# An adaLN transformer block on one core: the order of 2109 operations taken from a priority list, or from a table of the sequence itself

## The chip, the core and the metric

The kernel runs on one core of a Trainium2 chip. A core has a matrix engine (TensorE, PE in the profile, with its weight loads listed apart as PEld), a vector engine (VectorE, DVE), an activation engine (ScalarE, ACT), a general one (GpSimd, POOL), and a queue that mostly issues transfers (SyncE, SP). Each engine works through its own list of instructions strictly in order and waits on semaphores for the others. SBUF is the on-chip memory of 128 partitions, PSUM the accumulator of the matrix engine, in banks of 512 float32 columns.

The metric is the device time of one execution in microseconds (us). The kernel before takes 337.96 us, the median of three runs (336.16 to 338.79).

## The reference

The input x has 2048 tokens of 640 features, in bfloat16. A condition vector c gives six vectors of 640 by one product with a matrix `w_mod`: a shift, a scale and a gate for each of two layer norms.

```python
mod = (silu(c) @ w_mod).reshape(1, 6, 1, -1)
sa, ca, ga, sb, cb, gb = mod[:, 0], ..., mod[:, 5]
h = layernorm(x) * (1 + ca) + sa
x = x + ga * attention(h, wqkv, wo)
h = layernorm(x) * (1 + cb) + sb
x = x + gb * ((sigmoid(h @ w_gate) * (h @ w_up)) @ w_down)
```

The attention has 32 heads of 20 features, is causal, and a query sees the 256 last positions only. The second half has 1536 hidden features.

## The kernel before, in words

The tokens are cut into eight chunks `a` = 0..7 of 256 tokens (two blocks of 128). A chunk goes through these steps; each is a handful of operations of a program that the kernel first builds as a graph and then puts into an order:

- `x`: a block of x is loaded (by SP or ACT, line 603). Layer-norm statistics on DVE (L791, L793), the inverse root on POOL (L796, L798), the normalised block on DVE or POOL (L811, L808). In the first layer norm these operations carry the names `astats`, `apow`, `axh`, in the second `bstats`, `bpow`, `bxh`.
- `atr`, `btr`: the block is turned by a transposing DMA on SP (L818) and then scaled and shifted (`amodu`, `bmodu`, L826 and L827, on DVE, ACT or POOL), giving hT, and in the second half h2T. In chunks 0 and 1 the first turn is done by PE instead (`aptr`, evicted by `ahTe`, L849 and L850).
- `projq`, `projk`, `projv`: three projections of the turned block, in tiles of 320 columns, each five matmuls cut into pieces of two and three. A tile is evicted by ACT or DVE (`evqk`, `evv`, L884 and L885). q and k are turned by a transposing DMA (`qkt`), in chunks 0 and 1 by PE (`qtr`, evicted by `evqt`).
- `score`: 8 or 16 small matmuls into the tile S, which takes four PSUM banks and exists once. ACT takes the exponential of the whole tile (`exp`, L1005); POOL sets masked corners to zero (`mask`, L1013 and L1015). The next `score` needs S back, so it waits for the exponential before it.
- `pvs`: after six score sets (three in chunk 0) the products with V, into two neighbouring banks of M. In most places `pvs` is one PE operation together with the score that follows it. DVE turns, divides and turns back (`tr1`, `recip`, `divide`, `tr2`: L1052, L1057, L1059, L1061); four DMAs write the result to DRAM (`n_ow`), one or two read it back in the wanted layout (`oT`).
- `wo`: the output projection, added to x on DVE (`res1`, L1135), then the second layer norm.
- `mlpg`, `mlpu`: gate and up products over h2T, `tanh` on ACT (L1180), `glu` on DVE (L1182) into hh. `down`: the last product, added on DVE (`res2`, L1201), and `out`, the store.

Ahead of this stands the head: `w_mod` is loaded in quarters `wm0` to `wm3`, and c gives the modulation columns (`modA`, `modb`, `modc`, evicted at L753, L776). `warm` and `fill` are matmuls on zeros. `wos` and `wds` scale the loaded weights by the gates (L1228, L1163); `wd` and the others are loaded once. Part `wm0` and part `wm3` of `w_mod` are put where `wd` is loaded later.

PSUM holds S (four banks) and M, four banks that all other products share: a new tile of M waits until the eviction of the one that held the bank.

**What sets the order.** `Prog.op` records each operation with the engines that may do it, an assumed duration, and what it reads and writes. `Prog.schedule` (before) is a list scheduler: it keeps a simulated clock for each engine, takes the operations that could start soonest, and among those within 0.14 us (PE) or 0.04 us (others) of the earliest it picks the one with the smallest number in the list `PRIO`. It also picks one of the allowed engines and the buffer. The result is one fixed list for each engine; `Prog.emit` writes these lists out with a semaphore wait wherever an operation needs a result of another engine, a landed transfer, or a buffer. So on the chip every engine only follows its list, and an operation whose turn has come blocks all that stand behind it on that engine.

Nearly every PE instruction stands under one line of a helper, L705, and L706 for those with a tile position (scores and `pvs`). L686 and L697 are the `warm` and `fill` matmuls.

## Time and profile before

| what | us |
| --- | --- |
| median of three runs (lowest, highest) | 337.96 (336.16, 338.79) |
| span of the profiled execution | 333.9 |
| median less that span | 4.06 |
| PE busy, matmuls (L705 and L706 and warm-up) | 325.6 |
| ACT busy | 229.3 |
| PEld busy (beside PE) | 232.0 |
| DVE busy | 222.4 |
| POOL busy | 180.5 |
| 90 exponentials, L1005 | 169.1, mean 1.878 each |

The span goes from the first instruction of the program to its last; 4.06 us separate it from the median of the runs, which were not profiled. An engine is busy when it executes an instruction, not when it waits. The chain is followed back from the last instruction, at each step to what released it. A line of the chain or of the timeline gives the start and the duration in us, then engine, line and tiles (out<-in), and behind `<-` who ended the idle time before it.

### The profile page before, as it was taken

The numbers are of one execution on the slowest core, as the hardware profiler recorded it, in microseconds if no ns is written. First come the engines' busy times: TensorE is split into PE (matmuls) and PEld (weight loads), VectorE is DVE, ScalarE is ACT, GpSimd is POOL, SyncE is SP. The second block draws the span as 40 slices with busy tenths as digits, with TensorE's granted clock in tenths as the row PEclk, the third lists the DMA queues.
The fourth block names the chain that finished last, engine by engine and source line by source line (L and its number), as shares of the span: only waits on it lengthen the run. The fifth ranks groups of instructions, "written<-read, shape, count | busy, mean of one in ns | idle before, by whom it ended". The sixth has DMA issues, their size and how long they took to land.

```text
span 333.9 us, 10066 instructions
## 1 busy us (share of the span) xinstructions
PE 325.6 (98%) x4142; PEld 232.0 (69%) x4142; DVE 222.4 (67%) x445; ACT 229.3 (69%) x218; POOL 180.5 (54%) x259
## 2 busy tenths in 40 slices
PE   7899989998999999999999999999999999999996
PEld 2667646665786667766776776776776777887885
DVE  5389987999969845874486638465856295746323
ACT  1597977878768787888689967895695869221220
POOL 5038988996468764656565656665454667001000
PEclk9999999999999999999999999999999999999999
DMA  7999998984653773047125501501320303102101
GB/s 239 380 375 313 239 261 178 289 187 74 120 97 80 120 124 89 23 101 101 66 61 105 100 26 42 117 22 43 71 67 22 104 2 77 42 24 61 41 0 39
DMA packets 72694, 37.73 MB, mean 113 GB/s; under 512 B 46538, under 2 KB 71370, under 8 KB 72650
## 3 DMA queue, kind: packets, MB, share of 16 engines
q1 hardware_dynamic: 71056, 35.31, 43.9%
q10 hardware_dynamic: 1594, 1.80, 1.7%
q8 instruction: 32, 0.52, 0.6%
q14 instruction: 12, 0.10, 0.1%
HBM read 20.97 MB, written 5.24 MB: 79 GB/s over the span
## 4 chain that ended last, share of the span: by engine, by line
PE 86%; DVE 6%; DMA 3%; issue 2%; SPq 1%; ACT 0%; DVEq 0%
PE M L705 70%; PE S L706 8%; PE M L706 6%; DMA wd<-in_w_mod_dram 3%; PE S L686 2%; SPq L603 1%; DVE st L791 1%; DMA x<-in_A_x_dram 1%; DVE Tn L1059 1%; DVE T L1052 1%; DVE On L1061 1%; DVE x L811 1%; PE S L705 1%; DVE stg L885 1%; DVE h2T L827 0%
## 5 line engine op out<-in xcount | busy, mean ns | idle before, releaser
L1005 ACT ACTIVATE E<-S 128x2048 bf16<-128x2048 f32 x90 | 169.1, 1878 | 44.5 <-PE S L706 42.7
L1013 POOL TENSOR_SCALAR_AFFINE_SELECT E<-E 128x512 bf16<-128x512 bf16 (+2 forms) x90 | 78.2, 869 | 40.2 <-ACT E L1005 40.1
L1015 POOL TENSOR_SCALAR_AFFINE_SELECT E<-E 128x512 bf16<-128x512 bf16 (+1 forms) x84 | 68.5, 815 | 47.7 <-ACT E L1005 44.4
L705 PE MATMUL M<-h2T,wg 128*128 128x256 bf16 x480 | 64.8, 273 | 1.0 <-DVE h2T L827 1.0
L705 PE MATMUL M<-h2T,wu 128*128 128x256 bf16 x480 | 65.2, 273 | 0.0
L1182 DVE SCALAR_TENSOR_TENSOR hh<-sig,M 128x512 bf16<-128x512 f32 x48 | 32.6, 681 | 44.4 <-ACT sig L1180 24.4
L705 PE MATMUL M<-wd,hh 128*128 128x320 bf16 (+2 forms) x396 | 58.4, 295 | 0.0
L705 PEld LDWEIGHTS M<-h2T,wg 128*128 128x128 bf16 x480 | 45.0, 98 | 10.6 <-issue 2.3
L705 PEld LDWEIGHTS M<-h2T,wu 128*128 128x128 bf16 x480 | 45.3, 98 | 9.4 <-issue 3.0
L1180 ACT ACTIVATE sig<-M 128x512 f32<-128x512 f32 x48 | 28.3, 596 | 29.0 <-PE M L705 29.0
L705 PEld LDWEIGHTS M<-wd,hh 128*128 128x128 bf16 x396 | 37.1, 98 | 14.5 <-issue 1.5
L706 PE MATMUL S<-QT,KT 20*128 20x256 bf16 (+1 forms) x960 | 35.9, 245 | 0.2
L1201 DVE TENSOR_TENSOR x<-M,x 128x320 bf16<-128x320 f32 (+2 forms) x33 | 15.7, 479 | 23.4 <-PE M L705 22.9
L791 DVE BATCH_NORM_STATS2 st<-x 128x6 f32<-128x320 bf16 x64 | 28.3, 475 | 3.6 <-DMA x<-in_A_x_dram 3.5
L1052 DVE STREAM_TRANSPOSE T<-M 128x512 f32<-128x512 f32 x32 | 21.3, 697 | 12.7 <-PE S L706 12.0
L706 PEld LDWEIGHTS S<-QT,KT 20*128 20x128 bf16 x960 | 14.1, 92 | 20.1 <-ACT E L1005 12.1
L705 PE MATMUL M<-wk,hT 128*128 128x320 bf16 x160 | 26.6, 300 | 0.1
L705 PE MATMUL M<-wq,hT 128*128 128x320 bf16 x160 | 25.7, 299 | 0.2 <-issue 0.2
L705 PE MATMUL M<-wv,hT 128*128 128x320 bf16 x160 | 25.3, 300 | 0.1
L705 PE MATMUL M<-wo,oT 128*128 128x320 bf16 x160 | 24.1, 300 | 0.0
L706 PEld LDWEIGHTS M<-E,V 128*32 128x32 bf16 x960 | 20.0, 97 | 4.2 <-issue 2.6
L706 PE MATMUL M<-E,V 128*32 128x256 bf16 (+1 forms) x960 | 22.8, 246 | 0.2 <-issue 0.2
(78 smaller groups left out, 316.5 us busy)
## 6 DMA issues: line engine op xcount, KB each, us to landing
x<-in_A_x_dram SPq DMA_DIRECT2D x20, 160.0 KB
doc<-On SPq DMA_DIRECT2D x64, 40.0 KB
wd<-in_w_mod_dram SPq DMA_DIRECT2D x6, 320.0 KB
wd<-in_B_w_down_dram SPq DMA_DIRECT2D x4, 480.0 KB
wu<-in_w_mod_dram SPq DMA_DIRECT2D x5, 320.0 KB
out_dram<-x SPq DMA_DIRECT2D x10, 160.0 KB
oT<-doc SPq DMA_DIRECT2D x8, 192.0 KB
wg<-in_B_w_gate_dram SPq DMA_DIRECT2D x2, 576.0 KB
```

Of the source, the lines that this page charges most:

```text
L603: return e.dma_start(dst(), src())
L686: ins = e.matmul(p_S.aps[0][:, 3, :], Eall[:, 0, 0:128], Eall[:, 0, 128:640], start=True, stop=True)
L705: return e.matmul(o, l, r, start=st, stop=sp, skip_group_check=True)
L706: return e.matmul(o, l, r, start=st, stop=sp, tile_position=tp, skip_group_check=True)
L791: A("dve", lambda e, g, bi=bi, j=j: e.bn_stats(v(bi * 12 + j * 6, 6), src[bi].ap[:, j * 320:(j + 1) * 320]), 0.48, reads=[src[bi].r()], wr ...
L1005: A("act", lambda e, eng: e.activation(E.ap[:], Sp.ap[:], ACT.Exp, scale=SM_SCALE), 1.876, reads=[Sp.r()], writes=[E.r()], prio=3, tag=f"e ...
L1013: return e.affine_select(ap, ap, pattern=[[0, ap.shape[1]], [1, 128]], compare_op=ALU.is_ge, fill=0.0, base=0, channel_multiplier=-1)
L1015: return e.affine_select(ap, ap, pattern=[[0, ap.shape[1]], [-1, 128]], compare_op=ALU.is_ge, fill=0.0, base=-1, channel_multiplier=1)
L1052: A("dve", lambda e, g, h=h: e.transpose(T1.ap[:, 512 * h:512 * h + 512], X[h].ap), 0.694, reads=[X[h].r()], writes=[T1.r(h)], prio=3.5, t ...
L1180: A("act", lambda e, g, pg=pg, sg=sg: e.activation(sg.ap[:], pg.ap[:], ACT.Tanh, scale=0.5), c_act(512), reads=[pg.r()], writes=[sg.r()], ...
L1182: A("dve", lambda e, g, pu=pu, sg=sg, f0=f0: e.scalar_tensor_tensor(out=hh.ap[:, f0:f0 + 2, :], in0=sg.ap[:].rearrange("p (a b) -> p a b", ...
L1201: A("dve", lambda e, g, ps=ps, bi=bi, c0=c0, n=n: e.tensor_tensor(x1[bi].ap[:, c0:c0 + n], ps.ap[:, 0:n], x1[bi].ap[:, c0:c0 + n], op=ALU. ...
```

## The change

`PRIO` goes, and with it the choice by priority. In its place stands `PLAN`, a table with one number for each of the 2109 operations, in the order in which the scheduler is to place them: the number is 5 times the operation's number plus the engine's (pe, act, dve, pool, sp = 0 to 4). `schedule` walks through the table, and its simulated clock now only serves to choose the buffer of each tile (`place`). Some assumed figures of transfers change as well (a mixed turn between transposing and other transfers, the latency of the first loads and of transposes, the work of three loads); on the chip they can act only through the choice of buffers, since the order is in the table. The functions that issue instructions are the same.

```diff
-        o.prio = PRIO[self.seq] if self.seq < len(PRIO) else prio
+        o.prio = prio
...
-            return max(x.end + x.lat for x in ten.rel)
-
-        def slots_for(o):
...
+            return max(x.end + x.lat for x in ten.ops)
+
+        def take(t, s):
+            ten = t.pool.tenant[s]
+            t.prev = list(t.pool.init[s]) if ten is None else list(ten.rel)
+            t.slot = s
+            t.at = slot_time(t.pool, s)
+
+        def place(t):
+            n = len(t.pool.tenant)
+            free_at = [slot_time(t.pool, s) for s in range(n)]
+            if t.mate is not None:
+                best = min((max(free_at[s:s + 2]), s) for s in range(0, n, 2) if None not in free_at[s:s + 2])[1]
+                for x, s in ((t, best), (t.mate, best + 1)):
+                    take(x, s)
+                    t.pool.tenant[s] = x
+            else:
+                best = min((free_at[s], s) for s in range(n) if free_at[s] is not None)[1]
+                take(t, best)
+                t.pool.tenant[best] = t
+
+        assert sorted(x // 5 for x in PLAN) == list(range(len(self.ops)))
+        for code in PLAN:
+            o, e = self.ops[code // 5], ENGS[code % 5]
...
-PE_EPS = 0.14
-PRIO = [
-    237, 718, 740, 875, 142, 777, 323, 635, 239, 322, 238, 840, 25, 1100, 489, 421, 2052, 27, 111, 30, 29, 31, 28,
...
+PLAN = [
...
-MIXED = 0.39
+MIXED = 1.3
...
-    keep[0], keep[1] = load_x(p_x1, 0, 0), load_x(p_x1, 1, 0, eng="act")
+    keep[0], keep[1] = load_x(p_x1, 0, 0, dlat=2.95), load_x(p_x1, 1, 0, eng="act", dlat=2.95)
...
-    dma(lambda: wo[:], lambda: A_wo.rearrange("(t p) f -> p t f", p=128), 2.25, writes=[R_wo], prio=0.5, tag="wo")
+    dma(lambda: wo[:], lambda: A_wo.rearrange("(t p) f -> p t f", p=128), 2.15, writes=[R_wo], prio=0.5, tag="wo")
...
-        return A("sp", fn, dur, reads=reads, writes=writes, prio=prio, work=work, tag=tag, lat=0.08 + DSAFE, dlat=3.64 if work > 0.5 else 3.40)
+        return A("sp", fn, dur, reads=reads, writes=writes, prio=prio, work=work, tag=tag, lat=0.08 + DSAFE, dlat=3.35 if work > 0.5 else 3.25)
```

The table can be read by the operations' numbers. In the names used above, the lists of the engines then differ as follows at the places that matter below (the digit is the chunk, "x4" four pieces in a row, "|" only a help for the eye).

```
SP before, from the start:
x0 wm0x5 wq wm1 wkx2 x3 x2 wv wm1x2 x5 wm2 wm1 wq wm1 x4 wg0 x6 x7 wm2 wo wg0 wg1x2 atr2x2
n_ow_0x4 wu1x2 wu0 oT_0 wu0 | wm3x2 | x8 x9 atr3 qkt2 n_ow_0x4 ...
SP after:
wm0 x0 wm0x4 wq x2 wq wkx2 x5 x4 x3 wv wm1x5 wm2 wo x7 wm2 x6 | wm3x2 | wg1 wg0x2 atr2x2 wg1
wu1 wu0x2 n_ow_0 x9 x8 wd ...
ACT before: x1, c, tanh of c ...        ACT after: c, x1, tanh of c ...

PE before, from the start:
warmx4 ctr modA warmx3 aptr0 fill modA fill modA aptr0 modA fill modA fill aptr0x2 modA fill aptr0 projq0 ...
PE after:
ctr warmx7 modAx2 fill modAx2 fill aptr0x4 modAx2 fillx3 aptr0 projq0 ...
DVE before: ... astats0x5 c_col astats0 siluc silubc axh0x2 ...
DVE after:  ... c_col siluc silubc astats0x6 axh0x2 ...

PE before, from wo0 to mlpg0:
wo0x8 score1 projk3x3 projq3x2 projk3 score1 projq3x6 score1 projv3x2 projk3x2 projv3x3 score1 projk3x2
projv3x3 score2 projk4x6 projq4x2 pvs1 projv4x6 score2 projv4x2 projq4x5 score2 projq4 mlpg0
PE after:
wo0x4 projq3 wo0 score1 wo0x3 projq3 projk3 score1 projk3x2 projq3 projk3 projq3 score1 projq3x2 projv3
projk3x2 score1 projv3 projq3 projk3x2 projq3 projv3 score2 projv3x5 pvs1 mlpg0
DVE before, the second layer norm of chunk 0:
res1_0x2 bstats0 res1_0 bstats0x3 evqk3 bstats0x2 divide_1 evqk3x2 astats5x3 tr2_1 evqk3 astats5 evv3x2
astats5 evqk3 evv3 astats5 evv3 astats6x2 evqk4 astats6 evqk4 wds bxh0 wds bxh0
DVE after:
res1_0 recip_1 divide_1 res1_0x3 bstats0x6 tr2_1 evqk3x2 bxh0x2
POOL after, there: mask1 bpow0 mask1 bpow0 mask1        SP after, there: n_ow_1 atr4 btr0x2
```

(`ctr` turns c; `c_col`, `siluc` and `silubc` are the steps on DVE from it to the operand of `modA`, L673 to L677.) Of the 2109 operations 128 are on another engine than before, nearly all of them evictions and modulations that two or three engines may do; DVE has 437 operations instead of 445, POOL 260 instead of 247, ACT 212 instead of 217 without transfers.

## The prediction

> **What bounds the kernel now.** I read the page first: busy times, then the span in 40 slices.

> ```profile
> span 333.9 us, 10066 instructions
> PE 325.6 (98%) x4142; PEld 232.0 (69%) x4142; DVE 222.4 (67%) x445; ACT 229.3 (69%) x218; POOL 180.5 (54%) x259
> ...
> PE   7899989998999999999999999999999999999996
> ```

> PE is busy for 325.6 of 333.9 us, the next engine for 229.3. Whatever the order, the same 4142 matmuls remain, so only PE's 8.3 idle us (and waits too short to show as idle) can be won. Where they lie is told by PE's busy time in stretches (start:end, length, then PE busy and its instructions):

> ```profile
> 0.00:5.00 5.00, 3.28 (x8) 1.03 (x8) 2.41 (x9) 1.28 (x1) 3.29 (x25) 1.00 0.60 193
> 10.00:15.00 5.00, 4.16 (x50) 2.83 (x47) 1.45 (x4) 2.82 (x7) 0.00 (x0) 1.00 1.10 377
> 30.00:35.00 5.00, 4.64 (x63) 3.06 (x62) 5.00 (x10) 5.00 (x7) 4.20 (x5) 1.00 1.03 173
> 45.00:50.00 5.00, 3.71 (x32) 2.04 (x30) 3.48 (x10) 3.08 (x2) 4.66 (x6) 1.00 1.08 185
> 80.00:85.00 5.00, 4.02 (x42) 2.18 (x40) 5.00 (x10) 3.50 (x5) 3.12 (x3) 1.00 0.02 7
> 100.00:150.00 50.00, 50.00 (x676) 34.98 (x674) 37.12 (x77) 41.22 (x38) 33.12 (x45) 1.00 0.44 89
> ```

> From 85 us to the last matmul, PE's share is full. All that an order can win lies ahead of 85 us: 1.72 us before the first matmul, then 4.0 in holes; the last 2.5 us follow the last matmul. The waits of PE name the holes (total us, times, longest):

> ```profile
> PE M L705 <- DMA wd<-in_w_mod_dram: 1.3, 1, 1.3
> PE M L705 <- DVE h2T L827: 1.0, 2, 0.6
> PE M L705 <- DVE hT L850: 0.6, 1, 0.6
> PE M L705 <- DVE stg L885: 0.4, 1, 0.4
> ```

> Some waits hide in "busy", since a matmul's shown duration covers its way through the array. The chain shows the pattern of the attention: a score set, other matmuls, the next set.

> ```profile
> 124.81 0.34 PE S L706 x16
> 125.14 2.07 PE M L705 x18
> 127.22 0.33 PE S L706 x8
> ```

> S exists once and its exponential takes 1.878 us (mean of 90), so two sets lie never closer than 2.07 us of other work; this shortest value comes again and again. An order with less than that between two sets makes PE wait.

> **Part by part.** The sum goes against the span of 333.9 us; 4.06 us on top lead to the median of the runs.

> *Nothing for the bulk.* The table reorders pieces; the number of changes of PE between full, score and `pvs` form, counted in both lists, is 184 and 184. Evictions that move between ACT and DVE (128 operations in all) are covered by PE: DVE and ACT have a third of the span free. In 100 to 150 us, with 41.22 of 50 us of ACT busy, PE still lost nothing. I take 0, bounds -0.3 (PE's smallest holes) and +1.

> *The wait for `wm3`: -1.3.* Before, SP issues this part behind the four `n_ow_0`, and so behind DVE's `tr2_0`, which ends at 33.06 in the chain; its last issue is at 38.62, and the matmul on it starts at 47.06 instead of 45.77.

> ```profile
> 38.62 8.39 DMA wd<-in_w_mod_dram
> 47.06 1.12 PE M L705 x7
> ```

> After, SP has it directly behind x7, wm2 and x6, which wait only for PE's turns of chunk 1 (before, these ended at about 21). Even if it again takes the 8.39 us, it is there at some 33 us; PE comes to it after 26.8 us of matmuls counted from the first `projq0`, that is at 39. The row is that of the same transfer, so I take all of it; the other bound is 0.

> *The second layer norm of chunk 0: -0.8.* PE waits twice for h2T:

> ```profile
> 81.68 0.38 PE L705 MATMUL M<-h2T,wg 128*128 128x256 bf16 x2 [0.37 <-DVE h2T L827]
> ...
> 82.89 1.09 PE L705 MATMUL M<-h2T,wg 128*128 128x256 bf16 x8 [0.61 <-DVE h2T L827]
> ```

> Before, PE's list has 20.9 us of work between the last `wo0` piece and `mlpg0`, and the chain still was late: DVE did the last `res1` at 60.58 but `bxh0` (L811) only at 73.41, with casts, a division of 1.40 and a wait of 0.78 for x between them. After, PE has only 11.9 us there: 58 matmuls of 320 columns at 0.136, five score sets, one `pvs` of 1.43. But DVE's list is nearly straight. From the start of the last `wo0` piece: the piece and its hand-over 0.6, DVE not free for `res1` until 1.0, `res1` 0.45, statistics 2.3 (four of 0.475, two of 0.195): 4.3 us. On POOL 0.26, a mask of 0.87 to 1.1, the power 0.71: 6.3. `bxh0` 0.4: 6.7, the second one on DVE beside it. Two transposes of 1.22 in SP's queue: the second is issued at 7.9; from its issue to the first use (76.98 to 80.42) it took 3.4: 11.3. The modulation of two fifths 0.5, split over ACT and DVE: 11.8; the others by 12.4. So it just fits, with some 0.2 left of the 1.0: -0.8. Bounds: -1.0, and +7 if the chain is as slow as before (rival 1).

> *Score sets too close: +0.9.* Counted by matmul rows (0.136 for 320 columns, 0.109 for 256), the new list has places with less than those 2.07 us. Example: `wo0x3 projq3 projk3` between two `score1` is 12 matmuls, 1.63, with the change of form 1.73: 0.34 short. Summed over the list 1.7 us are short, with one place of 0.41 in chunk 0, two of 0.33 in chunk 1, one of 0.21 in chunk 2. The old list had 0.7 short, which its time holds already. Net +1.0; some of it falls on waits for an eviction anyway, so +0.9, bounds 0 and +1.0.

> *The head: -0.4.* c is now loaded first and c's small chain on DVE stands ahead of the statistics; on PE `ctr` stands ahead of all warm-up matmuls. It needs the identity, which POOL had at 3.62 before and now makes after a memset of 0.95 (of Tn) and one of 0.2 to 0.9 (nearest rows: DVE's 0.21, Tn's 0.95): 3.0 to 3.7. So PE starts 1.3 to 2.0 later than at 1.72. That is no loss by itself, for the first needed `modA` waits for its load anyway. The gain: after, the two last `modA` follow each other with no `fill` between, and all transfers ahead of them are the same, so the modulation that ended at 10.92 can end by 0.4 to 0.5 us earlier; and the first two evictions of hT run on ACT and DVE at once, 0.3 more. Against it:

> ```profile
> 1.72 3.59 PE L686 MATMUL S<-E 128*128 128x512 bf16 x8 [1.72 <-DVE E L681]
> 5.60 2.14 PE L686 MATMUL S<-E 128*128 128x512 bf16 x6
> ```

> Single matmuls of 512 columns step by 0.427 us up to 6.88 and by 0.217 from then on, 5.16 us after the first one. If the slow time is counted from the first matmul, it now lasts to 8.5; the fourteen warm-up matmuls alone then end at 8.9 instead of 8.3, the five `modA`, fills and turns (2.5 us of rows) at 11.5: +0.6. If it ends at 6.88 as before, -0.75. Between the two I take -0.4, nearer to the gain, since the loads set the last `modA`.

> [...]

> **Sum:** -1.3 -0.8 +0.9 -0.4 = -1.6. Span 332.3, time 336.4 us, 0.5% under the median. A change of about 1% is what a measurement here can tell from none: the three runs differ by 0.8%.

> **Rivals.** 1, slower: *h2T of chunk 0 comes late.* PE's list gives 9 us less to the chain than before (11.9 instead of 20.9), and everything behind `mlpg0` waits on PE in order. For it: the chain took 22 us before, transposes issued in that stage took long, and POOL's power stands behind a mask that waits for ACT. Against it: DVE's list has no load and no foreign division in the chain. If DVE and SP lose again the 7 us by which `res1` to `bxh0` (12.8) exceeded my 5.4, the 0.8 is gone and 7 come on top: 333.9 - 0.8 + 7 = 340.1, time 344. It decides from 5 us of lateness on (1.6 won plus 3.4, which is 1%). Chance 0.21.

> 2, faster: *PE's holes close wholly.* -0.75 (head) -1.3 -1.0 -0.4 (the wait for stg) -0.3 (the smallest holes) = -3.75, the short score sets falling on waits that both lists have: 330.2, time 334.2. For it: none of the holes is needed by the work. Against: the 1.7 short. Chance 0.22.

> 3, no change: *the won time is lost to evictions.* In 15 to 75 us ACT and DVE are near 4.5 to 5.0 of 5 us busy; M has four banks, and `pvs` needs two neighbours, free at once. One such wait is worth an exponential, 1.9, as an eviction behind it on ACT holds a bank. With that, 333.9 - 1.6 + 1.9 = 334.2, time 338.3. Chance 0.17.

> Forecast 0.40. Each case spreads by about 1% around its time. From these: faster by over 1% (under 334.6) 0.25, within 1% 0.54, slower (over 341.3) 0.21. The range reaches from a full gain less a little, 333.0, to the middle of rival 1, 342.5.

> **What would show it.** PE's wait for the `w_mod` load gone; first `projq0` at 11.9 instead of 12.26; `mlpg0` at about 71 instead of 81.68, with a wait for h2T under 0.3; waits of score weights for the exponential longer than 0.4 us near 22 and 60 us; PE full from 85 us on. It is wrong if PE waits over 2 us for h2T or for a bank, or if holes appear behind 85 us, where the list before had none and I have only counted, not followed, each engine.

## The result and the profile after

| what | before | after |
| --- | --- | --- |
| median of the runs, first comparison (us) | 337.8 (336.08 to 338.79, 6 runs) | 334.54 (333.99 to 334.97, 6 runs) |
| median, second comparison (the batch of `after_again`) | 336.19 (335.53 to 338.78, 23 runs) | 334.76 (333.31 to 335.99, 12 runs) |
| span of the profiled execution | 333.9 | 332.3 |
| time less span | 1.8 to 2.0 | 1.7 to 1.8 |

The ratio after to before is 0.9922, interval 0.9896 to 0.9949, in the first comparison and 0.9951 (0.9933 to 0.9970) in the second: a gain of 0.5 to 0.8%. The forecast was 336.4; the time is 1.9 us lower. The profiled execution of the changed kernel is the shortest of its six: their spans go from 332.3 to 333.2, with a median of 332.8.

The page of the changed kernel, busy times and the span in 40 slices:

```profile
span 332.3 us, 10064 instructions
...
PE 324.6 (98%) x4142; PEld 232.7 (70%) x4142; DVE 217.1 (65%) x437; ACT 226.3 (68%) x213; POOL 185.8 (56%) x272
...
PE   6998999999999999999999999999999999999997
```

PE's busy time in stretches (start:end, length, then PE busy and its instructions):

```profile
0.00:5.00 5.00, 1.95 (x6) 0.84 (x7) 2.20 (x7) 1.49 (x2) 2.68 (x12) 1.00 0.61 191
10.00:15.00 5.00, 4.88 (x54) 3.09 (x51) 3.77 (x9) 2.05 (x4) 0.00 (x0) 1.00 1.11 373
25.00:30.00 5.00, 4.04 (x99) 2.88 (x98) 4.27 (x10) 3.99 (x4) 4.41 (x4) 1.00 0.90 279
30.00:35.00 5.00, 5.00 (x67) 3.82 (x65) 4.36 (x13) 3.75 (x6) 3.71 (x4) 1.00 1.27 347
45.00:50.00 5.00, 5.00 (x57) 3.13 (x55) 4.97 (x10) 4.73 (x6) 3.95 (x6) 1.00 0.90 261
80.00:85.00 5.00, 5.00 (x57) 3.19 (x54) 2.17 (x6) 4.12 (x4) 3.88 (x7) 1.00 1.03 141
```

The holes at 45 and at 80 us (1.3 and 1.0 us before) are closed. A new one stands at 25 to 30. The waits of PE (total us, times, longest) name it:

```profile
PE M L617 <- POOL mhalf L561: 3.0, 1, 3.0
PE M L651 <- DMA hh<-in_w_mod_dram: 1.0, 1, 1.0
PE M L651 <- DVE hT L773: 0.3, 1, 0.3
PE M L651 <- DVE T L998: 0.2, 1, 0.2
```

The wait for `wm3` (tensor wd) and both waits for h2T are gone. The first line is the start, where PE waits for the identity, which POOL makes just ahead of mhalf. The second is new: `modc` needs the second part of `wm2` (tensor hh), whose load SP now issues behind x7, at 23.64 (21.93 before); it lands at 29.23. By the semaphore events of the trace 15 of its 16 parts had landed at 27.43, ahead of PE's turn at 28.3; PE waits for the last one.

To see short waits too, I set each PE operation's distance to the next against the shortest such distance of its form (below: "over the rows"). From the first `projq0` on, before loses 6.1 us so and after 4.9. (The measure is a rough one: it gives 1.2 less from there on, where the two spans, less the earlier `projq0`, differ by 0.9.) The large items: `wm3` 1.45 and h2T 0.54 + 0.77, only before; `wm2` 1.03, only after. Score sets at the shortest distance of 2.38 us cost 0.55 before and 1.2 after (0.40, 0.32 and 0.33 in the three worst places). The first `projq0` starts at 11.58 instead of 12.26. Behind 85 us no hole is to be seen in either.

### The profile page after: what moved, and what is told of

Same layout as the page of the kernel before. It is cut to its first block, busy times and chain, and to the rows that moved or that the text cites. A ratio compares the mean times of both kernels' runs of the same rounds, so it can differ in the third digit from the quotient of the medians.

```text
span 332.3 us, 10064 instructions
## 1 busy us (share of the span) xinstructions
PE 324.6 (98%) x4142; PEld 232.7 (70%) x4142; DVE 217.1 (65%) x437; ACT 226.3 (68%) x213; POOL 185.8 (56%) x272
## 4 chain that ended last, share of the span: by engine, by line
PE 93%; ACT 2%; DMA 2%; DVE 1%; POOL 1%; issue 1%; SPq 0%; POOLq 0%
PE M L651 76%; PE S L652 9%; PE M L652 6%; ACT E L951 2%; DMA hh<-in_w_mod_dram 2%; PE S L632 1%; DVE hT L773 1%; PE S L651 0%; PE S L643 0%; POOL Tn L572 0%; DVE T L998 0%; DVE QT L831 0%; POOL ident L558 0%; POOL stg L569 0%; SPq L549 0%
## 5 line engine op out<-in xcount | busy, mean ns | idle before, releaser
L961 POOL TENSOR_SCALAR_AFFINE_SELECT E<-E 128x512 bf16<-128x512 bf16 (+1 forms) x84 | 67.7, 813 | 56.6 <-ACT E L951 56.3
L959 POOL TENSOR_SCALAR_AFFINE_SELECT E<-E 128x512 bf16<-128x512 bf16 (+2 forms) x90 | 75.9, 854 | 17.4 <-ACT E L951 17.2
L651 PE MATMUL M<-h2T,wu 128*128 128x256 bf16 x480 | 68.5, 273 | 0.2 <-DVE T L998 0.2
L651 PE MATMUL M<-h2T,wg 128*128 128x256 bf16 x480 | 67.8, 273 | 0.0
L651 PE MATMUL M<-wd,hh 128*128 128x320 bf16 (+2 forms) x396 | 57.7, 295 | 0.0
L998 DVE STREAM_TRANSPOSE T<-M 128x512 f32<-128x512 f32 x32 | 21.0, 691 | 12.4 <-PE S L652 11.2
L651 PE MATMUL M<-wq,hT 128*128 128x320 bf16 x160 | 27.4, 299 | 0.5 <-DVE hT L773 0.3
L651 PE MATMUL M<-wk,hT 128*128 128x320 bf16 x160 | 27.4, 300 | 0.0
L651 PE MATMUL M<-wv,hT 128*128 128x320 bf16 x160 | 26.0, 300 | 0.0
L831 DVE CAST stg<-M 128x320 bf16<-128x320 f32 x38 | 17.7, 483 | 10.9 <-PE M L651 10.9
L742 POOL TENSOR_SCALAR st<-st 128x2 f32<-128x2 f32 x16 | 3.7, 234 | 34.9 <-DVE st L739 34.6
(79 smaller groups left out, 335.3 us busy)
```

Source lines behind the costliest of these rows:

```text
L651: return e.matmul(o, l, r, start=st, stop=sp, skip_group_check=True)
L742: A("pool", lambda e, g: e.tensor_scalar(v(28, n), var(), EPS, None, op0=ALU.add), 0.2, reads=[st.r(("m", bi)) for bi in range(n)], writes ...
L831: return e.tensor_copy(dst(), src())
L959: return e.affine_select(ap, ap, pattern=[[0, ap.shape[1]], [1, 128]], compare_op=ALU.is_ge, fill=0.0, base=0, channel_multiplier=-1)
L961: return e.affine_select(ap, ap, pattern=[[0, ap.shape[1]], [-1, 128]], compare_op=ALU.is_ge, fill=0.0, base=-1, channel_multiplier=1)
L998: A("dve", lambda e, g, h=h: e.transpose(T1.ap[:, 512 * h:512 * h + 512], X[h].ap), 0.694, reads=[X[h].r()], writes=[T1.r(h)], prio=3.5, t ...
```

## The experiments

In all edits below except `b_banks` each buffer is held to the one that the edited kernel uses, so that only the order changes. Names that begin with b_ edit the kernel before, with a_ the changed one. The rows `b_table` to `b_ln2` ran beside the first batch of before, `b_wm3b` to `a_oldhead` beside the second, the rest beside the third, each batch on a chip of its own; a ratio compares within its batch. The "low-clock" column counts executions whose mean granted clock (the share of its full clock at which PE was let run) was 0.990 to 0.995 instead of 0.999 or 1.0; the spans are medians of the others.

| run | median time | ratio to before | span at full clock (lowest, highest) | low-clock |
| --- | --- | --- | --- | --- |
| before, three batches | 336.58, 336.37, 336.19 | | 334.25, 334.2, 334.2 (333.6, 335.5) | 20 of 81 |
| b_table | 336.35 | 0.9994 [0.9967, 1.0021] | 334.5 (333.9, 335.1) | 2 of 12 |
| b_banks | 336.50 | 0.9988 [0.9963, 1.0013] | 334.5 (334.0, 335.1) | 2 of 12 |
| b_wm3 | 336.17 | 0.9977 [0.9951, 1.0003] | 334.3 (333.5, 335.5) | 0 of 12 |
| b_ln2 | 335.07 | 0.9945 [0.9917, 0.9974] | 332.95 (332.3, 333.6) | 2 of 12 |
| b_wm3b | 334.54 | 0.9933 [0.9908, 0.9959] | 332.6 (332.3, 333.1) | 0 of 7 |
| a_wm2 | 335.11 | 0.9944 [0.9923, 0.9966] | 333.4 (332.3, 333.9) | 0 of 11 |
| a_lnlate | 340.77 | 1.0116 [1.0083, 1.0148] | none | 6 of 6 |
| a_oldhead | 335.43 | 0.9963 [0.9943, 0.9982] | 333.7 (333.0, 334.5) | 0 of 12 |
| after_again | 334.76 | 0.9951 [0.9933, 0.9970] | 333.05 (331.6, 334.3) | 0 of 12 |
| a_space2 | 336.34 | 1.0003 [0.9981, 1.0025] | 334.65 (333.7, 336.7) | 0 of 12 |
| b_both | 332.85 | 0.9894 [0.9864, 0.9925] | 330.95 (330.9, 331.4) | 0 of 6 |
| b_bothhead | 333.61 | 0.9919 [0.9890, 0.9949] | 331.55 (331.1, 332.4) | 0 of 6 |

### Is it the order at all, and where do the runs of before differ?

`b_table` is the order and the buffers of before, in the new code (`pin` is a list with the buffer of each tile).

```diff
 PLAN = [
-    3, 57, 81, 114, 78, 91, 62, 89, 222, 99, 68, 104, 8, 13, 263, 109, 28, 195, 225, 202, 206, 212, 230, 217, 119,
+    91, 62, 23, 89, 3, 81, 72, 114, 53, 222, 104, 43, 57, 225, 48, 99, 67, 33, 230, 263, 78, 109, 235, 367, 38, 372,
...
-            best = min((free_at[s], s) for s in range(n) if free_at[s] is not None)[1]
+            best = pin[t]
```

> The order and the buffers of the kernel before, written as a table in the new code: every engine's list is that of before. Both theories expect a ratio of 1.000 (0.997 to 1.003), about 337.8 us. What it is to tell apart is where the runs of this order differ (336.1 to 338.8 in six runs). Theory A, they differ inside the span, in waits of the first 85 us: time less span is the same in each run (about 1.7 us, as in all runs of the new order) and the spans go from 334.4 to 337.1. Theory B, they differ outside of the span: the spans all lie within 0.5 us of 333.9 and time less span goes from 2.2 to 4.9.

Measured: ratio 0.9994, so table and code carry nothing. Time less span is 1.8 to 2.0 in every execution, and the spans go from 333.9 to 336.5: theory A. They also fall in two heaps. With a granted clock of 1.0 they end at 335.1, with 0.995 they begin at 336.0. In the 81 executions of before, 20 have the lower clock (spans from 335.7 on, the others up to 335.5).

`b_banks` is the same order with the buffers that the new figures choose.

```diff
-            best = pin[t]
+            best = min((free_at[s], s) for s in range(n) if free_at[s] is not None)[1]
```

> The order of the kernel before, but with the buffers that the new figures choose for it (96 tiles of M lie in another PSUM bank). Theory A, banks carry nothing: 337.8, ratio 0.998 to 1.002. Rival, the new choice of banks is a part of the gain (fewer waits for an eviction): 0.5 to 1.5 us less, 336.3 to 337.3, and PE's stalls by missing banks (33.1 and 75.8 us in the old profile, 0.7 together) gone.

Measured: 336.50, ratio 0.9988. The stalls at 33.1 and 75.8 us stay (0.42 and 0.37 over the rows). The choice of banks is no part of the gain.

### The wait for wm3

First the two loads ahead of the parts of `w_gate`:

```diff
 SP: ... x6 x7 wm2 wo
+wm3 wm3
 wg0 wg1 wg1 atr2 atr2 n_ow_0x4 wu1x2 wu0 oT_0 wu0
-wm3 wm3
 x8 x9 ...
```

> The kernel before with one edit: the two loads of wm3 stand behind wo in SP's queue, ahead of the four parts of w_gate, and no more behind the writes of n_ow_0. Theory A, the wait is a loss of its own: PE's 1.3 us for w_mod at 45.8 is gone and the span is 1.3 to 1.5 shorter than that of before in the same batch; if this load is also what differs by run, the spread of the runs falls from 2.7 to about 1 us. Rival, the wait is only handed on (h2T at 81 us, or the exponentials, end the same stretch): under 0.4 us less.

Measured: PE waits for `wm3` no more, and the span is 334.3, as before: the rival held. The waits of PE now name the exponential (2.0 us together), and ACT's timeline (start, duration, operation, and the idle time before it with its releaser) shows why:

```profile
33.80 1.94 ACT L980 ACTIVATE E<-S 128x2048 bf16<-128x2048 f32 x1
35.55 0.67 ACT L859 ACTIVATE KT<-M 128x512 bf16<-128x512 f32 x1
38.18 0.60 ACT L801 ACTIVATE hT<-hT,mA 128x256 bf16<-128x256 bf16 x1 [1.95 <-DMA hT<-x]
38.68 1.86 ACT L980 ACTIVATE E<-S 128x2048 bf16<-128x2048 f32 x1
```

ACT comes to the modulation of chunk 2 and waits 1.95 us for its transposes, with the next exponential behind it. The first of the two is issued at 29.66, as before (29.50), but lands 7.98 us later instead of 3.99. The second, on which the chain puts ACT's wait, takes 5.98 instead of 3.37:

```profile
32.11 5.98 DMA hT<-x
```

The two loads put ahead of them take 2.3 us to land one after the other (29.72 to 31.97); that is the larger part of the 4 us, and the rest is not traced. PE then waits 1.37 over the rows for that exponential, in place of 1.45 for `wm3`. (The profiled execution, at 335.4, is 1.1 above the median and has longer waits at 70 and 77 us as well.)

Then the same loads behind these transposes:

```diff
 SP: ... wm2 wo wg0 wg1 wg1 atr2 atr2
+wm3 wm3
 n_ow_0x4 wu1x2 wu0 oT_0 wu0
-wm3 wm3
 x8 x9 ...
```

> The kernel before with one edit: the two loads of wm3 stand in SP's queue behind the transposes of chunk 2 and ahead of the four writes n_ow_0, so behind the loads and transposes that the exponentials of 38 us hung on when they stood further ahead. Theory A, PE's wait for w_mod is a loss of its own, where the load takes nothing's place: spans of 332.6 to 333.0, 1.3 to 1.6 under the 334.3 that the undisturbed executions of before show, and none of the executions with a granted clock of 0.995, which 13 of 35 of before had and which were about 1.8 us longer; so a median of 334.5 and a ratio of 0.994 or less. Rival 1, the wait is handed on again as in the first edit: 334.3, and only the clock is cured. Rival 2, the lower clock has nothing to do with this wait: a third of the runs shows it again.

Measured: span 332.6, which is 1.6 less than before, and no execution with a low clock. Theory A: where the load takes nothing's place, the whole wait is won. This one move in one queue gives 334.54, the same as the change of the whole order.

### The second layer norm of chunk 0

```diff
 POOL: ... mask1 mask1 mask1 bpow0
+bpow0
 mask1 amodu4x2 ... apow5
-bpow0
 DVE: ... astats5x3 tr2_1
+bxh0x2
 evqk3 astats5 ... evqk4 wds
-bxh0
 wds
-bxh0
 wds tr1_1 ...
+bmodu0x4
 recip_1 ... wds
-bmodu0x4
 SP: ... qkt3x3
+btr0x2
 n_ow_1x3 qkt3 n_ow_1 qkt4
-btr0x2
 oT_1 ...
```

> The kernel before with one edit: in the second layer norm of chunk 0 the power stands directly behind the statistics on POOL, the two bxh0 directly behind tr2_1 on DVE, the two btr0 ahead of the n_ow_1 on SP, and the bmodu0 ahead of the reciprocal on DVE. PE's order stays. Theory A: both waits of PE for h2T (0.54 and 0.77 over the rows at 80.7 and 81.9) go, 1.0 to 1.3 us less than before in the same batch. Rival, what was moved past (three evictions of chunk 3, and the masks on POOL) comes late in its place: 0 to 0.4 less, or up to 1 more.

Measured: span 332.95, 1.3 less: theory A. Over the rows 0.54 and 0.77 are gone, and three short waits at 69 to 76 us (0.6 together); 0.41 is new at 70 us.

The profiled execution of this run has the low clock, and so shows where it comes from. The half clock lasts 3.41 us in it, from 49.00 to 52.42, and begins 44.36 us, 13.00 times its own length, behind the point at which the matmuls' steps halve at the start (4.64 here, 6.88 in before). The stretches below have this length and are counted from that point. The last columns are the granted clock, the DMA share and GB/s.

```profile
42.18:45.59 3.41, 3.41 (x45) 2.13 (x34) 3.36 (x6) 3.41 (x5) 2.25 (x5) 1.00 1.04 358
45.59:49.00 3.41, 1.47 (x14) 0.70 (x15) 1.66 (x4) 1.19 (x1) 3.08 (x5) 1.00 1.31 211
49.00:52.42 3.42, 3.42 (x20) 1.75 (x18) 1.58 (x6) 1.88 (x1) 2.24 (x3) 0.50 0.88 192
52.42:55.83 3.41, 3.41 (x44) 1.87 (x43) 2.18 (x5) 2.40 (x3) 1.20 (x3) 1.00 0.33 85
```

Here the wait for `wm3` lasted 1.9 us and fell wholly into one stretch, in which PE was busy for 1.47 of 3.41 us. In the next stretch the clock is 0.50: 20 matmuls instead of some 44. That costs 1.7 us, half of the stretch. In the profile of `b_table` the same wait lasted 1.5 us; PE had 1.89 us of work in the stretch, and the clock stayed:

```profile
44.42:47.84 3.42, 1.89 (x19) 0.93 (x18) 2.17 (x4) 2.51 (x4) 2.98 (x4) 1.00 1.35 282
```

The length of the wait does not decide alone. In the profile of `b_banks` it lasted 1.86 us, but a border of two stretches, counted in the same way, fell into it, so that PE was busy for 2.22 and 2.75 us in them, and the clock stayed:

```profile
43.55:46.97 3.42, 2.22 (x22) 1.10 (x19) 2.74 (x5) 3.09 (x4) 2.40 (x3) 1.00 1.64 346
```

Over all runs, the kernels that keep this wait show the low clock in 26 of 117 executions, those in which it is gone (and `a_lnlate` aside) in 0 of 84. So the low clock of before is a consequence of this one wait.

### The places of the changed kernel

The new wait:

```diff
 SP: ... wm1x5 wm2
+wm2
 wo x7
-wm2
 x6 wm3x2 ...
```

> The changed kernel with one edit: the second load of wm2 stands ahead of wo in SP's queue and no more behind x7, whose issue waits for PE's turns of chunk 1. Theory A: the new wait of PE of 1.0 us at 28 to 29 us goes, and nothing takes its place since wo is first needed ten us later: span 331.2 to 331.5, time 333.5 (1.0 under the changed kernel). Rival, handed on to the scores, which by then are a full exponential apart: 0.3 or less won.

Measured: the load lands at 24.49, PE waits for it no more, and the span is 333.4, no less than the changed kernel's 333.05 or its first six executions' 332.8. The win was handed on, as the rival said, but by another road. PE has 0.9 us of wait for "DVE QT" ahead of `pvs` at 37 us. DVE's and POOL's timelines around it, first in the changed kernel's first profile, a line from each engine:

```profile
36.18 0.81 DVE L1005 TENSOR_TENSOR Tn<-T,Dr 128x640 bf16<-128x640 f32 x1
...
36.17 2.07 POOL L1174 TENSOR_TENSOR wo<-wo,gbc 128x640 bf16<-128x640 bf16 x1
```

and in `a_wm2`:

```profile
35.76 2.01 DVE L1034 TENSOR_TENSOR Tn<-T,Dr 128x640 bf16<-128x640 f32 x1
...
35.69 1.39 POOL L1203 TENSOR_TENSOR wo<-wo,gbc 128x640 bf16<-128x640 bf16 x1
```

Where POOL starts 0.01 us ahead, DVE's division takes 0.81 and POOL's product 2.07; where POOL is 0.07 us ahead, POOL takes 1.39 and the division 2.01. So each time one of the two has the length that it has elsewhere in the changed kernel (the division 0.81 at 109.47 us, with POOL idle; POOL's other product of this kind 1.39, at 27.99), and the other is 1.2 or 0.7 us longer. In both profiles the pair is through 2.07 to 2.08 us after its first start. The eviction behind the division, for which PE waits, is 1.2 us late where the division is the longer one. That the one instruction holds up the other is read from these rows and not tested: no run moves POOL's product away.

The changed kernel once more, without an edit:

> The changed kernel itself once more, on the chip of the runs beside it. Theory A: spans of 332.3 to 333.2, time less span 1.7 and no execution with a clock of 0.995, since its longest wait behind the head is 1.0 us: 334.5. Against the old order's 336.4 here that is a ratio of 0.994, with the larger gain of the first measurement (0.992) coming from the number of low-clock runs of before in it. Rival: the changed kernel has the same spread and the same low-clock runs, only fewer were seen.

Measured: 334.76; no low clock in 12 more executions; the spans spread over 2.7 us, three times what theory A gave. Its profile shows the same as `a_wm2` without the edit. `wm2`, issued at 23.83, landed already at 27.74 instead of 29.23; PE did not wait for it, the division took 2.00, and the wait at `pvs` came to 0.96 over the rows. So this stretch costs 1 us on either road in the profiled executions, and which one is taken differs by execution.

Rival 1 of the prediction, brought about by an edit:

```diff
 DVE: ... tr2_1 evqk3x2
-bxh0x2
 wds evv3 astats5x6 evqk3x2 evv3 wds
+bxh0x2
 bmodu0x2 tr1_1 ...
```

> The changed kernel with one edit: the two bxh0 of the second layer norm of chunk 0 stand on DVE 4.9 us later, behind the statistics of chunk 5 and the last wds ahead of the modulation. The profile shows 1.1 us between the landing of h2T and the modulation, so the chain theory (rival 1 of the prediction, PE's list has no cover left here) expects mlpg0 late by 3.0 to 3.8 us and the span longer by as much: 335.5 to 336.5. If a wait of PE of more than 2 us also turns its clock down for a window of 3.4 us, half of the runs or more show 0.995 and 1.7 us more: median 338 to 339.5. If the order takes the delay up elsewhere: under 1 us, 335.5.

Measured: 340.77, all six executions with a low clock, the spans 5.7 to 6.8 above 333.05. In the profile PE waits 4.1 us for h2T and 0.6 for the next part,

```profile
77.07 0.38 PE L680 MATMUL M<-h2T,wg 128*128 128x256 bf16 x2 [4.14 <-DVE h2T L802]
```

and the clock falls again in the stretch behind the one with nearly no work:

```profile
70.97:74.38 3.41, 1.83 (x72) 1.48 (x72) 1.02 (x3) 0.35 (x2) 2.91 (x5) 1.00 0.43 53
74.38:77.79 3.41, 0.38 (x2) 0.13 (x2) 1.46 (x4) 1.46 (x3) 0.00 (x0) 1.00 0.62 122
77.79:81.21 3.42, 3.15 (x19) 1.98 (x23) 2.79 (x4) 2.20 (x3) 1.47 (x3) 0.50 0.88 169
```

The delay became longer than the 4.9 us that I had meant: the first bxh0 starts at 71.20 and PE's `pvs1` at 71.10, in the changed kernel at 64.35 and 70.16, so it is 5.9 later. Of these, 4.7 appear as waits of PE, and the rest is about the 1.1 us that lay between the landing of h2T and its modulation. PE's list has no more cover than that, and in the profile the half clock costs 1.7 on top. Three of the executions show a clock of 0.99 instead of 0.995; their spans (338.7 to 339.8) are no longer than those of the other three (338.7 to 339.4).

The head of before in the changed kernel:

```diff
 PE:
-ctr warmx7 modAx2 fill modAx2 fill aptr0x4 modAx2 fillx3 aptr0
+warmx4 ctr modA warmx3 aptr0 fill modA fill modA aptr0 modA fill modA fill aptr0x2 modA fill aptr0
 projq0 ...
 ACT:
-c x1 tanh
+x1 c tanh
 SP:
-wm0 x0
+x0 wm0
 wm0x4 ...
 DVE:
-c_col siluc silubc astats0x6
+astats0x5 c_col astats0 siluc silubc
 axh0x2 ...
```

> The changed kernel with the head of before: PE's first 24 operations, DVE's list up to the evicted modulation, the first three operations of ACT and the first two loads of SP in the order of before; POOL as in the changed kernel. If the head is worth what the profiles show (first projq0 at 11.58 in place of 12.26): 0.5 to 0.8 us longer than the changed kernel, 335.1 to 335.3. By the step of the prediction: 0.4 longer, 334.9. If the head only fills time that a load sets: under 0.2.

Measured: span 333.7, that is 0.65 to 0.9 over the changed kernel (other batches, so not closer). The exchange of heads is worth this much here. Its profile has the first `projq0` at 12.53 (11.58 and 11.76 in the two of the changed kernel), and also a wait of 0.9 for DVE's reciprocal that neither of those two lists, so not all of it need be the start.

The score sets of chunk 1:

```diff
 PE: pvs1
-wo0x4 projq3 wo0 score1 wo0x3 projq3 projk3 score1
+wo0x2 score1 wo0x2 projq3 wo0x3 score1 wo0 projq3 projk3x2
-projk3x2 projq3 projk3 projq3 score1 projq3x2 projv3 projk3x2 score1
+projk3 projq3 score1 projk3 projq3x3 projv3 projk3 score1
 ...
```

> The changed kernel with one edit on PE's list alone: between pvs1 of chunk 1 and mlpg0 the five score sets stand up to two pieces of wo0 or of a projection earlier, so that at least 2.48 us of work by the rows lies between any two (before the edit three gaps lay at the 2.38 at which the rows show PE waiting). By the prediction's step on score sets these three places cost 0.7 us (0.32 + 0.06 + 0.33 over the rows), and 0.5 to 0.9 with the bank waits beside them: the span 0.5 to 0.9 shorter, 333.6 to 334.0. Rival, the evictions set this stretch: within 0.2 of the changed kernel.

Measured: 1.6 us longer. More than half of that is a mistake of mine that the timeline of PE shows (start, duration, operation, idle time before it and its releaser):

```profile
55.52 1.50 PE L681 MATMUL M<-E,V 128*32 128x256 bf16 x64
56.96 0.40 PE L681 MATMUL S<-QT,KT 20*128 20x256 bf16 x8
57.72 0.70 PE L680 MATMUL M<-wo,oT 128*128 128x320 bf16 x4 [0.37 <-DMA oT<-doc]
59.34 0.40 PE L681 MATMUL S<-QT,KT 20*128 20x128 bf16 x16 [0.91 <-ACT E L980]
```

`pvs1` carries a score set itself (the second line), so the set that I moved up came 2.38 us behind that one, with only four matmuls between: PE waited 0.91. Another wait of 0.37 stands before it, for oT; it lies ahead of the first place that the edit changes, so it belongs to this execution, whose span of 335.7 is 1.05 above the median. A third, of 0.51 for the exponential, stands at 71 us. The run confirms the 2.38 us, and says nothing on whether wider gaps there would win; that stays open.

### Both moves together

`b_both` has the edits of `b_wm3b` and `b_ln2`; `b_bothhead` has the head of the changed kernel in addition (the reverse of the diff of `a_oldhead`, and POOL's `Tn`, `stg` and identity first). The SP lines are for both, those of PE and POOL for the second alone; POOL and DVE have the edits of `b_ln2` too.

```diff
 SP:
+wm3x2
 n_ow_0x4 wu1x2 wu0 oT_0 wu0
-wm3x2
 ...
+btr0x2
 n_ow_1x3 qkt3 n_ow_1 qkt4
-btr0x2
 PE:
-warmx4 ctr modA warmx3 ...
+ctr warmx7 modAx2 ...
 POOL:
-V V V V V E Tn V V ident ...
+Tn stg ident mhalf E V ...
```

> The kernel before with the two edits that won alone: wm3 ahead of the n_ow_0 in SP's queue, and the second layer norm of chunk 0 moved up. If both are losses of their own (1.6 and 1.3): spans about 331.4, time 333.3, 1.2 under the changed kernel. If the second one is a consequence of the first or is handed on: 332.6, 334.5, as with the first alone. No low-clock run in either case.

> The same with the head of the changed kernel in addition: c first on ACT, wm0 ahead of x0 on SP, ctr ahead of all warm-up matmuls, c's chain ahead of the statistics on DVE, the identity early on POOL, the order of modA and turns. If the head is worth what its exchange in the changed kernel showed (0.9): spans about 330.5, time 332.4, the best of all. If the head's gain is given back by DVE further on: 333.3.

Measured: `b_both` takes 332.85, 1.1% less than before (0.9894, interval 0.9864 to 0.9925), and its slowest run (333.27) is below the fastest of the changed kernel in that batch (333.31). Its page and its stretches, with 1.2 us less of holes in 45 to 50 than before and none in 80 to 85:

```profile
span 331.0 us, 10066 instructions
...
PE   6899999999999999999999999999999999999996
```

```profile
45.00:50.00 5.00, 4.90 (x54) 2.84 (x52) 3.87 (x11) 3.89 (x3) 4.66 (x6) 1.00 1.11 179
80.00:85.00 5.00, 5.00 (x63) 3.65 (x62) 5.00 (x10) 4.81 (x5) 3.44 (x5) 1.00 0.36 72
```

`b_bothhead` takes 333.61, 0.8 more than without the new head (0.6 in the span). The first `projq0` starts 0.46 earlier in its profile (11.76 for 12.22), but 0.27 of it is given back at 47.6 us and 0.32 at 76.5, and its spans spread over 1.3 us where those of `b_both` spread over 0.5.

## Why the prediction was right, and where it was wrong

The range and the class held: 334.5 to 334.8 lies in 333.0 to 342.5, and the ratio is within 1% of none. The likeliest time, 336.4, was 1.9 too high.

**The step that failed: "4.06 us on top lead to the median of the runs".** The sum gave a span of 332.3, and the profile shows 332.3; that they agree to the digit is luck, for it is the shortest of the six, and the medians of the spans at full clock are 332.8 and 333.05. But time less span is 1.7 to 2.1 us in every execution of every kernel here whose span was recorded. The rest of the 4.06 was no constant: the profiled execution of before was a quick one, with its clock whole. In the first batch executions of before with the low clock have a median span of 336.2 against 334.25 for the others, 2 us more. In the one such execution that was profiled, that of `b_ln2`, it is a longer `wm3` wait and the half clock after it, and both go with the wait. That the two long ones of the three runs that I had (337.96, 338.79) were of this kind is inferred, for their clock was not recorded; four of the six runs of before in the first comparison are that long, against 20 of 81 later, and why so many stays open. I took the wait at its price in one execution, 1.3, and missed that half a clock can follow it, for 1.7 more in the profile of `b_ln2`. At the second comparison, where 3 of 23 executions of before had the low clock, the medians differ by 1.4, close to the 1.6 of the sum.

I had weighed the clock for the head alone. That it falls again later is shown by two profiles: in `b_ln2` after a stretch of 3.41 us in which a wait of 1.9 us left PE busy for 43% (1.47 us), in `a_lnlate` after one with 11% (0.38). After 54% (1.83 us in `a_lnlate`) and 55% (1.89 in `b_table`) it stayed. What lies between 43 and 54% no run shows. Nor did the start have one length in every execution: the matmuls' steps halved 5.16 us after the first matmul in before, 2.9 after it in `b_ln2`, and 3.8 after it in the changed kernel, where single matmuls of 512 columns step by 0.43 us up to 6.53 and by 0.21 from 6.85 on. That is near the 6.88 of before, the better of the two cases between which I took the head.

**wm3, -1.3: right, with a lucky neighbour.** The load in its old place cost 1.45 over the rows. My step took for granted that an early load is free. `b_wm3` shows that it is not: ahead of the transposes it wins nothing. In the changed kernel it also stands ahead of them, and there the modulations on ACT stand behind later exponentials, which my step did not name as the cover.

**The second layer norm, -0.8: right in kind, too small.** It is worth 1.3 alone and 1.65 on top of the other (332.6 to 330.95, in two batches). I had forecast that it "just fits, with some 0.2 left". There is 1.1 left: h2T lands at 69.16, and the modulation starts at 70.27, when ACT and DVE come to it. `mlpg0` started at 71.92 (I said about 71).

**Score sets too close, +0.9: right in sign by the rows.** They give +0.65 net. No run isolates it.

**The head, -0.4: right in sign for this order only.** The first `projq0` came 0.68 earlier (11.58, I said 11.9), and the exchange costs 0.65 to 0.9 there; in `b_bothhead` the new head makes the kernel slower by 0.8.

**Not in the sum: the road through `wm2` or through DVE's division, +1.0.** I followed SP's order past x7 for `wm3`, where the delay was harmless, and did not look who needs `wm2`, which stands in the same place. In the first profile this wait of 1.03 took what the layer norm (0.5), the head (0.3) and the score sets (0.25) were better than my numbers, so the span came out right by errors that cancel.

**Nothing for the bulk: right.** Behind 85 us neither kernel has a hole.

**The rivals.** The first one (h2T late) did not come, but its price was real: `a_lnlate` pays 5.7 to 6.8 us for a delay of 5.9. The second (the holes close wholly) gave 334.2 and so came nearest to the time, for a reason that is not the one that the runs show: the span is 332.3 and not 330.2. The third had evictions eat the gain; what ate part of it was a load or, by the rows, a division on DVE that took 2.0 us in place of 0.81 beside a product on POOL.

## What to carry to other kernels

Where time and profiled span differ by more than in other runs, ask what varies between executions, and look at the granted clock of each, before adding the difference as a constant. Price a wait of the matmul engine like the one for `wm3` at its length plus the cost of a half clock behind it times the chance of one. Here that cost was 1.7 us in the profile of `b_ln2`, behind a wait of 1.9 us (behind one of 1.5 in `b_table` and one of 1.86 in `b_banks` the clock stayed), and the chance 26 of 117. Removing the wait was worth more than one quick profile shows: 1.8 in the medians (`b_wm3b`), for a wait of 1.45. And a list of two thousand operations that was ordered anew can be matched by moving two loads: find the few waits first, and when a load is moved up, look at the transposes behind it (in `b_wm3` one landed 4 us later).
